# Attention plus linear attention on one core: loads in order of use, the last output projection accumulated early, a kept PSUM bank, VectorE steps kept back, and new step prices in the program's own scheduler

## The chip, the cores and the metric

The kernel runs on one core of one Trainium2 chip. The metric is device time in microseconds (us), the median of several executions. Faster or slower needs 2%. A core has five engines with separate instruction streams: TensorE (PE, matmuls into PSUM), VectorE (DVE), ScalarE (ACT), GpSimd (Pool) and SyncE (SP, which here issues loads and stores). The program divides PSUM into eight banks of 128 x 512 fp32.

## The reference, cut to what matters

```
def _A_ref(x, wqkv, wo):                      # softmax attention, 32 heads of 16
    qkv = (x @ wqkv) ...                      # x: 2048 x 512
    p = softmax(einsum("bhqd,bhkd->bhqk", q, k) * Dh**-0.5)
    o = einsum("bhqk,bhkd->bhqd", p, v)
    return o @ wo
def _B_ref(x, wqkv, wo):                      # linear attention with phi(t) = elu-like map
    kv = einsum("bhsd,bhse->bhde", phi(k), v); z = sum_s phi(k)
    return ((phi(q) @ kv) / (phi(q) @ z)) @ wo
g = sigmoid((x * gate_w).sum(-1, keepdims=True))
return g * a + (1 - g) * b
```

Softmax attention needs 32 x 2048 x 2048 exponentials. They come as 2048 tiles of 128 keys by 512 queries of one head.

## The kernel before

The program writes its own schedule. While it is being built, a small scheduler keeps a clock for each engine, prices each step, and appends instructions to the engines' streams in the order that its clocks suggest. Each stream keeps the order in which it was appended, and its steps wait for those of other engines by semaphores. So a wrong price does not slow an instruction down; it puts it at a place where something else has to wait for it.

There are 32 rounds (a quarter of the queries, four heads at a time). In a round, PE makes score tiles, ACT takes exponentials of three and two tiles in turn, and PE multiplies the results with V into one accumulating bank.

```
gsets = [(0, 1, 2), (3, 4)]                   # PSUM banks of ACT's tiles: three, then two
op(AC, lambda: nc.scalar.activation(PT[:, slot, 0:512 * n], ps[...], ACT.Exp, scale=SCALE), ...)
cur_units[0] = 64 * last[0] + 4 * last[1] + last[2] + 1    # progress: ACT's tiles only, 64 a round
```

VectorE takes some blocks of four tiles (one key block) off ACT. It evicts scores from banks 5 and 6 to integers, then computes the exponential by four chain steps on 128 x 2048 elements; PE multiplies three partial results with V:

```
op(DV, ... tensor_scalar(Lb[...], src, S1A, S1B, op0=ALU.mult, op1=ALU.add), cost=0.158 + 0.533 * n)   # n = 1 or 2 tiles
CH = [0.685, 0.685, 1.216, 0.685]             # the four chain steps (and, and, bf16 multiply, add)
def op(E, ...):                               # how VectorE is priced
    if E is DV:
        ev = E.add(fn, ..., cost=cost - 0.035, lag=0.035)
```

Everything else (projections for K, V, Q, the linear attention, the gate, the output projections) are tasks that use the same two banks 5 and 6 and start when the progress reaches their number `nb`. The gate ends in sixteen tiny copies, and an output projection is eight matmuls into one bank and an eviction:

```
for j in range(4):
    for a in range(4):
        op(DV, ... tensor_copy(gv[32*j:32*j+32, :, a], g0[32*a:32*a+32, :]), ..., cost=0.08)
def t_out(qc, q):                             # ops_: 4 products of part B, then 4 of part A
    for h in range(4):
        yield ("pe", rd, ..., 2)
        pe([mm(BK[b], ops_[k][0], ops_[k][1], start=(k == 0), stop=(k == 7)) for k in (2*h, 2*h+1)], ...)
    op(DV, ... tensor_copy(outt[:, sl, :], BK[b]), ..., cost=0.69)
add(("out", qc, q), t_out(qc, q), ..., max(17.2 + 3.0*qc + 3.0, 8*qc + 8.1) + 0.3*q if qc < 3 else 31.9, ...)
```

Where PE would stand idle by the scheduler's clock, it issues filler matmuls on a buffer of zeros (`sb_warm`), meant to keep PE's clock up.

The softmax here doesn't subtract the row's maximum and nothing guards it: scores larger than these inputs give would overflow.

## Time and profile before

| | before |
|---|---|
| median of three runs | 797.72 us (797.4 to 798.54) |
| span of the profiled run | 800.8 us |
| ACT busy | 764.0 us |
| first exponential starts | 17.75 us |
| last exponential ends | 788.7 us |

The following lines are of the page of the kernel before: span, busy time of each engine, the chain of waits by engine, and three groups of instructions (line, engine, operation, output <- inputs, count, then busy us and mean ns, then idle time just before them and what ended it). PEld are PE's weight loads; ACTq and SPq, here and below, are the loads and stores that ACT and SP issue.

```profile
span 800.8 us, 18062 instructions
...
PE 745.8 (93%) x7910; PEld 229.4 (29%) x7969; DVE 693.0 (87%) x979; ACT 764.0 (95%) x694; POOL 7.6 (1%) x35
...
ACT 84%; PE 8%; DVE 4%; issue 2%; DMA 1%; ACTq 0%; DVEq 0%
...
L840 ACT ACTIVATE sb_PT<-ps 128x1536 bf16<-128x1536 f32 (+1 forms) x659 | 757.0, 1413 | 14.7 <-PE ps L363 14.5
...
L1061 DVE TENSOR_SCALAR sb_Lb<-ps 128x512 uint16<-128x512 f32 (+1 forms) x282 | 256.4, 910 | 61.3 <-PE ps L363 57.6
...
L1088 DVE TENSOR_TENSOR sb_Xb<-sb_Xb,sb_Lb 128x2048 bf16<-128x2048 bf16 x100 | 121.6, 1216 | 0.0
```

ACT is busy from the first exponential to the last with few gaps, and the chain that ended last runs through it for 84% of the span. L840 are the exponentials (L363, in the lines below, is the helper that every matmul goes through); their idle time (14.5 us behind PE) contains the 6.3 us before the first. L1088 runs once in each of VectorE's blocks, so its count, 100, is the number of blocks. L1061 is the score eviction that opens them: VectorE stands 57.6 us waiting for PE there.

Three places outside the steady stream cost time. The first is the start (timeline: start, duration, engine, line, operation, count, and in brackets the idle time before it and its releaser):

```profile
1.81 7.00 ACTq L307 DMA_DIRECT2D sb_OT<-in_A_wqkv_dram  x2
...
12.26 3.57 PE L363 MATMUL ps<-sb_xT,sb_OT 128*128 128x512 bf16 x8 [6.03 <-DMA sb_OT<-in_A_wqkv_dram]
...
17.75 19.53 ACT L840 ACTIVATE sb_PT<-ps 128x1536 bf16<-128x1536 f32 x17 [6.29 <-PE ps L363]
```

The first K projection waits until 12.26 us for two small weight tiles (they borrow the space of `sb_OT`); issuing those two loads took ACT's queue 7.0 us. The second place is the tail, from the timeline of the end:

```profile
768.88 19.85 ACT L840 ACTIVATE sb_PT<-ps 128x1536 bf16<-128x1536 f32 x17
...
789.98 0.59 PE L363 MATMUL ps<-sb_phiK,sb_OT 128*128 128x512 bf16 x2
...
792.09 0.60 PE L363 MATMUL ps<-sb_phiK,sb_OT 128*128 128x512 bf16 x2 [1.52 <-DVE sb_OT L947]
...
797.91 0.69 DVE L647 CAST sb_wA<-ps 128x512 bf16<-128x512 f32 x1 [1.03 <-PE ps L363]
```

The last exponential ends at 788.7 us. Then VectorE normalizes (`sb_OT` is done at 792.0 us), and only after that PE runs most of the last four projections, with an eviction behind each. The third place is two groups of gaps in ACT's stream, here one of them in ACT's timeline:

```profile
50.62 1.02 ACT L840 ACTIVATE sb_PT<-ps 128x1024 bf16<-128x1024 f32 x1 [1.97 <-PE ps L363]
52.40 1.45 ACT L840 ACTIVATE sb_PT<-ps 128x1536 bf16<-128x1536 f32 x1 [0.76 <-PE ps L363]
```

### The profile page before, as it was taken

What the parts mean: (1) busy time and instruction counts of PE and PEld (TensorE: products, weight loads), DVE (VectorE), ACT (ScalarE), POOL (GpSimd) and SP (SyncE); (2) the same over time, 40 slices, a digit from 0 to 9 for tenths busy, and PEclk for the clock granted to TensorE, in tenths of its full rate; (3) what the DMA queues carried; (4) which work ended last, traced back from release to release, by engine and by line L of the source; (5) the groups of instructions that cost most, each with busy time, mean ns of one, the idle gap of its engine ahead of it and who ended that gap; (6) DMA issues with size and microseconds to landing.
All of it is one profiled execution on the core that took longest, in us unless ns stands there. A gap on an engine that the chain in (4) does not pass through costs nothing.

```text
span 800.8 us, 18062 instructions
## 1 busy us (share of the span) xinstructions
PE 745.8 (93%) x7910; PEld 229.4 (29%) x7969; DVE 693.0 (87%) x979; ACT 764.0 (95%) x694; POOL 7.6 (1%) x35
## 2 busy tenths in 40 slices
PE   6989999999999999999999999999999999999997
PEld 2422322222222222232222223222322332233222
DVE  3278899999999989998989999987889899799995
ACT  1989999999999999999999999998999999999993
POOL 3000000000000000000000000000000000000000
PEclk9999999999999999999999999997999999999999
DMA  9000000000000000102001000000001000100000
GB/s 231 20 1 8 2 7 2 8 2 8 1 4 6 2 7 2 35 2 56 5 1 61 2 8 12 17 29 7 13 17 30 11 14 16 34 8 14 16 1 27
DMA packets 30782, 14.93 MB, mean 19 GB/s; under 512 B 18544, under 2 KB 30704, under 8 KB 30704
## 3 DMA queue, kind: packets, MB, share of 16 engines
q1 hardware_dynamic: 26512, 11.95, 5.7%
q10 hardware_dynamic: 4192, 1.84, 1.1%
q8 instruction: 62, 1.02, 0.5%
q14 instruction: 16, 0.13, 0.0%
HBM read 6.55 MB, written 2.10 MB: 11 GB/s over the span
## 4 chain that ended last, share of the span: by engine, by line
ACT 84%; PE 8%; DVE 4%; issue 2%; DMA 1%; ACTq 0%; DVEq 0%
ACT sb_PT L840 82%; PE ps L363 8%; ACT sb_ebuf L529 2%; DVE sb_Lb L1061 1%; DMA sb_OT<-in_A_wqkv_dram 1%; DVE sb_gT L521 0%; DVE sb_Xb L1082 0%; DVE sb_Xb L1088 0%; DVE sb_U L928 0%; DVE sb_Eb L1085 0%; DVE sb_phiK L533 0%; DVE sb_Lb L1091 0%; ACTq L307 0%; DVE sb_rden L940 0%; DVE sb_OT L947 0%
## 5 line engine op out<-in xcount | busy, mean ns | idle before, releaser
L840 ACT ACTIVATE sb_PT<-ps 128x1536 bf16<-128x1536 f32 (+1 forms) x659 | 757.0, 1413 | 14.7 <-PE ps L363 14.5
L363 PE MATMUL ps<-sb_QP,sb_KT 32*128 32x512 bf16 x2048 | 307.3, 387 | 27.6 <-ACT sb_PT L840 17.2
L1061 DVE TENSOR_SCALAR sb_Lb<-ps 128x512 uint16<-128x512 f32 (+1 forms) x282 | 256.4, 910 | 61.3 <-PE ps L363 57.6
L363 PEld LDWEIGHTS ps<-sb_QP,sb_KT 32*128 32x128 bf16 x2048 | 76.7, 91 | 289.2 <-ACT sb_PT L840 225.0
L363 PE MATMUL ps<-sb_PT,sb_V 128*17 128x512 bf16 x1648 | 156.1, 387 | 1.4 <-ACT sb_PT L840 1.1
L363 PE MATMUL ps<-sb_warm 128*17 128x512 bf16 (+8 forms) x2190 | 154.4, 344 | 1.6 <-POOL sb_dummy L387 1.3
L1088 DVE TENSOR_TENSOR sb_Xb<-sb_Xb,sb_Lb 128x2048 bf16<-128x2048 bf16 x100 | 121.6, 1216 | 0.0
L1082 DVE TENSOR_SCALAR sb_Xb<-sb_Lb 128x2048 uint16<-128x2048 uint16 x100 | 68.7, 687 | 1.3
L1091 DVE TENSOR_SCALAR sb_Lb<-sb_Lb 128x2048 uint16<-128x2048 uint16 x100 | 68.5, 685 | 0.0
L1085 DVE TENSOR_SCALAR sb_Eb<-sb_Lb 128x2048 uint16<-128x2048 uint16 x100 | 68.3, 683 | 0.0
L363 PEld LDWEIGHTS ps<-sb_warm 128*17 128x17 bf16 (+1 forms) x2193 | 50.3, 90 | 58.0 <-issue 31.3
L363 PEld LDWEIGHTS ps<-sb_PT,sb_V 128*17 128x17 bf16 x1648 | 37.4, 87 | 97.7 <-issue 90.5
L363 PE MATMUL ps<-sb_Lb,sb_V 128*17 128x512 bf16 x400 | 39.2, 383 | 0.1
L363 PE MATMUL ps<-sb_Xb,sb_V 128*17 128x512 bf16 x400 | 39.0, 381 | 0.1
L363 PE MATMUL ps<-sb_Eb,sb_V 128*17 128x512 bf16 x400 | 39.0, 380 | 0.0
L363 PE MATMUL ps<-sb_xT,sb_wA 128*128 128x512 bf16 x89 | 26.8, 382 | 4.3 <-issue 1.9
L928 DVE STREAM_TRANSPOSE sb_U<-ps 128x512 f32<-128x512 f32 x32 | 22.7, 709 | 4.3 <-PE ps L363 4.1
L529 ACT ACTIVATE sb_ebuf<-ps 128x512 bf16<-128x512 f32 x32 | 25.3, 791 | 0.0
L363 PE MATMUL ps<-sb_wA,sb_xT 128*128 128x128 bf16 (+1 forms) x128 | 20.4, 285 | 2.7 <-DVE sb_Lb L1061 2.7
L453 DVE CAST sb_KT<-ps 128x512 bf16<-128x512 f32 x16 | 11.0, 686 | 9.8 <-PE ps L363 9.7
L363 PE MATMUL ps<-sb_phiK,sb_OT 128*128 128x512 bf16 x63 | 17.7, 382 | 1.7 <-DVE sb_OT L947 1.5
L363 PE MATMUL ps<-sb_wBx,sb_xT 128*128 128x512 bf16 x52 | 16.1, 382 | 2.2 <-issue 1.4
(79 smaller groups left out, 303.1 us busy)
## 6 DMA issues: line engine op xcount, KB each, us to landing
out_dram<-sb_wA SPq DMA_DIRECT2D x16, 128.0 KB, 1.7
sb_QP<-sb_QT SPq DMA_DIRECT2D x120, 16.0 KB, 1.8
sb_xnat<-in_A_x_dram ACTq DMA_DIRECT2D x2, 512.0 KB, 5.2
sb_wA<-in_A_wqkv_dram SPq DMA_DIRECT2D x2, 512.0 KB, 6.6
sb_wBx<-in_B_wqkv_dram SPq DMA_DIRECT2D x2, 512.0 KB, 5.9
sb_xnat<-in_A_x_dram SPq DMA_DIRECT2D x2, 512.0 KB, 3.9
sb_phiK<-sb_wA SPq DMA_TRANSPOSE x64, 2.2
sb_wA<-in_A_wqkv_dram ACTq DMA_DIRECT2D x1, 512.0 KB, 6.2
```

Source lines behind the costliest of these rows:

```text
L363: return lambda: nc.tensor.matmul(o, lhsT=l, rhs=r, start=start, stop=stop, skip_group_check=sg)
L453: op(DV, lambda: nc.vector.tensor_copy(KT[:, t8, 512 * t:512 * (t + 1)], BK[b]), reads=[r_bk[b]], writes=[r_KT[t8][t]], cost=0.69)
L529: op(AC, lambda: nc.scalar.activation(ebuf[:, s, :], BK[b], ACT.Exp), reads=[r_bk[b]], writes=[r_e[s]], cost=0.48)
L840: op(AC, lambda: nc.scalar.activation(PT[:, slot, 0:512 * n], ps[:, 512 * set_[0]:512 * (set_[0] + n)], ACT.Exp, scale=SCALE), reads=wr, w ...
L928: op(DV, lambda: nc.vector.transpose(U[:, par, :], acc), reads=[r_acc], writes=[r_U[par]], cost=0.71)
L1061: op(DV, lambda: nc.vector.tensor_scalar(Lb[:, sl, 512 * k:512 * (k + n)], src, S1A, S1B, op0=ALU.mult, op1=ALU.add), reads=[r_bk[b] for b ...
L1082: op(DV, lambda: nc.vector.tensor_scalar(X, L, 0x7F, 0x3F00, op0=ALU.bitwise_and, op1=ALU.bitwise_or), reads=[rl], writes=[rx], cost=CH[0])
L1085: ev = op(DV, lambda: nc.vector.tensor_scalar(E_, L, 0xFF80, None, op0=ALU.bitwise_and), reads=[rl], writes=[re_], cost=CH[1])
L1088: ev = op(DV, lambda: nc.vector.tensor_tensor(xb, xb, lb, ALU.mult), reads=[rx, rl], writes=[rx], cost=CH[2])
L1091: ev = op(DV, lambda: nc.vector.tensor_scalar(L, L, float(EXP_SH), None, op0=ALU.add), reads=[rl], writes=[rl], cost=CH[3])
```

## The change

Its intent is fivefold. (1) What the first exponential needs (a quarter of x, two 128-column weight tiles) is loaded first, each part under its own semaphore, and two memsets on VectorE are put off until after the first K and Q. (2) The last four output projections may accumulate all products but the last before the last normalization, and half of them are evicted by ACT. (3) When a task is due, VectorE's blocks leave one of the two banks free. (4) A chain step is kept back while VectorE's next score tile is in the making, so that it can fill the wait. (5) VectorE's steps get new prices: shorter pitch, with a delay between dependent steps. Due times of second-round work move as well, the gate among them (from progress 0.6 to 1.9), and the wait for the gate moves from the end of a round into the normalization. The diff, cut to its core:

```
-                ev = E.add(fn, _deps_for(E, reads, writes), cost=cost - 0.035, lag=0.035)
+                ev = E.add(fn, _deps_for(E, reads, writes), cost=max(cost - 0.084, 0.05), lag=min(0.084, cost - 0.05))
... (and 0.034 us between dependent steps of one engine)
-        for hh in range(2):
-            dma(xnat[:, 8 * hh:8 * hh + 8, :], ..., E=AC)             # two loads of 512 KB
-        dma(wA0[:, 0], ..., "w0", writes=[r_wA0], E=AC)
-        dma(wA0[:, 1], ..., "w0", writes=[r_wA0], E=AC)
+        load_xn(0, AC, 3.0)                                           # 256 KB
+        dma(wA0[:, 0], ..., "w0k", writes=[r_wA0[0]], E=AC, lat=4)
+        dma(wA0[:, 1], ..., "w0q", writes=[r_wA0[1]], E=AC, lat=4.5)
+        load_xT(0, 0, 3.6); load_xT(0, 1, 4.9) ...                    # the rest behind, on SP
-        op(DV, lambda: nc.vector.memset(QP[:], 0.0), ...)             # memsets at the start
-        op(DV, lambda: nc.vector.memset(V[:]...[:, :, Dh:Dh + 1], 1.0), ...)
...
             for h in range(4):
+                last = qc == NQC - 1 and h == 3
+                for kk in ([[6], [7]] if last else [[2 * h, 2 * h + 1]]):
+                    if kk == [7]:
+                        yield ("wait", ("pair", 8 * qc + 7))          # the last normalization
...
+            if qc == NQC - 1 and q % 2:
+                op(AC, lambda: nc.scalar.copy(outt[:, sl, :], BK[b]), ...)
...
+            if not held and pressed():                                # a due task waits for a bank
+                free = free[1:]
...
-            add(("V1", tb), t_v1(tb), 0.9 + 0.05 * (15 - tb), 0.45 + 0.06 * (15 - tb), pre=XT)
-        add(("gate",), t_gate(), 0.6, 0.5, pre=XT)
+            add(("V1", tb), t_v1(tb), V1D + 0.05 * (15 - tb), V1N + V1S * (15 - tb), pre=XT)   # .7, .3, .05
+        add(("gate",), t_gate(), GD, GN, pre=XT)                                            # 1.9, 1.5
...
         need(("Q", 0, 0))
+        op(DV, lambda: nc.vector.memset(QP[:, 1:3], 0.0), ...)
+        op(DV, lambda: nc.vector.memset(V[:]...[:, :, Dh:Dh + 1], 1.0), ...)
...
+            if apos[0] >= NR - 1 and dst["cur"] is None and progress() > TAILP:   # 31.5
+                maxhold[0] = 2
...
+                elif dst["cur"] is not None and lastd[0] and len(chainq) < 2:
+                    cands.append((max(now, DV.clock + CHG), 0.6, 0.0, chain_op, None))
```

## The prediction

> **What bounds the kernel.** ScalarE's exponentials: busy table, ACT 764 of 800.8 us; chain of waits, 82% the 659 exponentials. A three-plus-two pair of score tiles occupies ACT for 2.26 us (timeline, 770 to 782 us); a tile costs 0.459 us (757.0 us for 1648). VectorE computes the other 400 tiles, as 100 blocks of four. Time can come from four places: before the first exponential (17.75 us), after the last (788.7 to 800.8 us), ACT's gaps between (8.4 us), or more blocks on VectorE (each takes 4 x 0.459 = 1.84 us from ACT).
>
> **Start.** PE waits 6.0 us for two small weight tiles behind two 512 KB loads; issuing them blocks ACT's queue for 7.0 us, and K starts at 12.26 us. The change loads the first quarter of x and each weight under its own semaphore, the rest behind. It frees VectorE's masks from Pool's chain (4.6 us wait). I expect data at about 6 us, K and Q at half clock as now (0.43 us a matmul), the first exponential at about 11 us. The Trainium skill (DMA: Bandwidth & Descriptors, Issuing engines are not separate DMA queues) says SP's and ACT's loads interleave on the same 16 engines, so bytes ahead matter, not the issuer; this trace can't yet show it. Worth 6.5 us, all critical.
>
> **Tail.** Transpose and normalization (789.2 to 792.0 us) stay. Then come 16 output matmuls with four 0.69 us evictions until 798.6 us, and the last store. With seven of eight products accumulated ahead, four matmuls remain and two pairs of evictions, ACT beside DVE: worth 4.5 us.
>
> **Gaps.** ACT loses 4.2 us at 48 to 56 us and 3.9 us at 550 to 564 us. Both follow a hole in PE's work (2.7 us behind the gate's copies, 3.24 us on DVE; 1.4 us), and the granted clock then is 0.5. The Trainium skill (TensorE: Matmul & The Clock Gate, What's actually happening) puts such halving after an idle window of about 3.4 us; these holes are shorter, though work around them is thin. The kept bank and later gate should remove part; the gate's copies are still scheduled too cheap (0.08 against 0.2 us). I take 3 us.
>
> **VectorE's share.** DVE waits 57.6 us for PE before score evictions, some 50 us of it in the steady part. Holding chain steps back fills those waits. The scheduler's new pitch for DVE steps (0.60 and 1.13 us) equals the trace's; the old (0.65 and 1.18) was slow, so it should claim more. If 30 us of waits are filled, at 5.2 us of DVE a block plus 1.84 us of shortening, 30/7.0 = 4 more blocks: 8 us. Kept banks give some back as single evictions (0.69 us for one tile, 1.22 for two).
>
> **Sum.** 6.5 + 4.5 + 3 + 8 = 22 us: 775.7 us, range 766 to 787. Faster by over 2% (below 781.8 us): 0.74; same 0.25; slower 0.01.
>
> **What would show it.** First exponential at 10 to 12 us; last exponential to end 7.5 instead of 12.1 us; ACT gaps under 6 us; 103 to 105 blocks (count of the 128x2048 multiply), score evictions waiting 20 to 35 us for PE.
>
> **What would make it wrong.** Blocks not rising, claims being limited by banks or PE (93% busy); new half-clock stretches; the second round's V, K or Q late because their weights load last; first loads landing after 6 us.

## The result, and the profile after

The changed kernel took 792.27 us (median of four, 791.6 to 792.87), the kernel before in the same rounds 798.13 us (797.4 to 798.81). The ratio is 0.9927, with a 95% interval of 0.9909 to 0.9944: 0.7% faster, "same" by the 2% rule, and outside the predicted range. Here and below a ratio is fast runs alone, set against runs of the other kernel in the same rounds, so not quite the ratio of the medians quoted.

The same lines of the page after:

```profile
span 790.4 us, 17903 instructions
...
PE 743.7 (94%) x7815; PEld 227.3 (29%) x7877; DVE 701.7 (89%) x1009; ACT 760.6 (96%) x692; POOL 7.6 (1%) x35
...
ACT 73%; PE 16%; DVE 7%; issue 3%; DMA 1%; SPq 0%
...
L874 ACT ACTIVATE sb_PT<-ps 128x1536 bf16<-128x1536 f32 (+1 forms) x655 | 752.3, 1420 | 16.6 <-PE ps L364 16.0
...
L1115 DVE TENSOR_SCALAR sb_Lb<-ps 128x512 uint16<-128x512 f32 (+1 forms) x302 | 264.8, 878 | 47.8 <-PE ps L364 46.0
...
L1142 DVE TENSOR_TENSOR sb_Xb<-sb_Xb,sb_Lb 128x2048 bf16<-128x2048 bf16 x103 | 125.1, 1214 | 0.0
```

103 blocks instead of 100, and a shorter wait of the score evictions. But ACT's share of the chain fell from 84 to 73% and PE's rose from 8 to 16%: more of what ended last went through PE. The start, in the timeline after:

```profile
1.21 1.08 ACTq L308 DMA_DIRECT2D sb_OT<-in_A_wqkv_dram  x2
...
6.59 1.89 PE L364 MATMUL ps<-sb_xT,sb_OT 128*128 128x512 bf16 x8 [0.89 <-DMA sb_xT<-in_A_x_dram]
...
9.76 3.71 ACT L874 ACTIVATE sb_PT<-ps 128x1536 bf16<-128x1536 f32 x3 [5.94 <-PE ps L364]
...
12.70 0.48 DVE L1241 MEMSET sb_V<- 128x512 bf16 x1 [1.70 <-issue]
...
14.52 1.02 ACT L874 ACTIVATE sb_PT<-ps 128x1024 bf16<-128x1024 f32 x1 [1.05 <-PE ps L364]
```

The same two weight loads are issued in 1.08 us instead of 7.0, K's eight matmuls start at 6.59 us and take 1.89 us (12.26 and 3.57 us before), and the first exponential starts at 9.76 us. But after three exponentials ACT stands 1.05 us: VectorE's put-off memset of V's ones column ends only at 13.2 us, and the first V eviction and PE queue behind it. Gaps of ACT in the second round, in its timeline, and the same stretch by windows of 5 us (busy us and count of each engine, then the granted PE clock, 1.00 being full, then DMA share and GB/s):

```profile
94.10 2.36 ACT L874 ACTIVATE sb_PT<-ps 128x1536 bf16<-128x1536 f32 x2 [1.64 <-PE ps L364]
97.44 2.52 ACT L874 ACTIVATE sb_PT<-ps 128x1536 bf16<-128x1536 f32 x2 [0.97 <-PE ps L364]
101.51 2.53 ACT L874 ACTIVATE sb_PT<-ps 128x1536 bf16<-128x1536 f32 x2 [1.56 <-PE ps L364]
104.89 11.40 ACT L874 ACTIVATE sb_PT<-ps 128x1536 bf16<-128x1536 f32 x10 [0.85 <-PE ps L364]
```

```profile
90.00:95.00 5.00, 2.95 (x24) 0.73 (x24) 4.43 (x19) 3.37 (x4) 0.00 (x0) 0.92 0.00 0
95.00:100.00 5.00, 4.11 (x22) 0.76 (x21) 3.66 (x7) 3.94 (x4) 0.00 (x0) 0.50 0.00 0
100.00:105.00 5.00, 5.00 (x36) 0.97 (x36) 4.30 (x6) 2.59 (x3) 0.00 (x0) 0.55 0.01 3
```

That is the gate stall of the kernel before, at another place: a hole in PE's work first (2.95 us busy of 5), then ten microseconds at half clock in which PE is busy throughout or nearly so and ACT starves. Of ACT's 5.0 us, 1.64 stand directly behind the hole, the rest in the half-clock stretch. The tail, in the timeline after:

```profile
764.25 14.15 ACT L874 ACTIVATE sb_PT<-ps 128x1536 bf16<-128x1536 f32 x13 [0.63 <-PE ps L364]
...
779.87 0.81 PE L364 MATMUL ps<-sb_phiK,sb_OT 128*128 128x512 bf16 x3
...
781.98 0.39 PE L364 MATMUL ps<-sb_phiK,sb_OT 128*128 128x512 bf16 x1 [1.30 <-DVE sb_OT L983]
782.21 1.03 PE L364 MATMUL ps<-sb_phiK 128*128 128x512 bf16 x4
...
786.52 1.03 PE L364 MATMUL ps<-sb_phiK,sb_OT 128*128 128x512 bf16 x4
787.59 0.59 ACT L664 CAST sb_wA<-ps 128x512 bf16<-128x512 f32 x1 [2.87 <-PE ps L364]
```

Only the first of four projections was accumulated ahead. After the normalization PE still runs 25 matmuls, against 26 before. The last exponential ends at 778.4 us and the program at 790.4 us.

The span is summed up in the next table. "Before again" is a second profile of the kernel before, from the experiments; the first one was a slow execution (802.6 us, while the timed runs of those rounds took 797.4 to 798.8 us; over all rounds, 10 of the 26 timed runs took over 800 us). Gaps are ACT's idle stretches before exponentials after the first one, as its timeline lists them.

| us | first profile of before | before again | after | after minus before again |
|---|---|---|---|---|
| until the first exponential | 17.75 | 18.32 | 9.76 | -8.6 |
| exponentials, busy | 757.0 | 756.1 | 752.3 | -3.8 |
| ACT's gaps | 8.2 | 4.35 | 10.1 | +5.7 |
| last exponential to the end | 12.1 | 12.1 | 12.0 | -0.1 |
| the rest (other ACT work) | 5.7 | 5.8 | 6.3 | +0.4 |
| span | 800.8 | 796.7 | 790.4 | -6.3 |

So the start delivered more than expected, the extra blocks about half, the tail nothing, and the gaps took back two thirds of the start.

### The profile page after: what moved, and what is told of

The parts are those of the page before. It is cut to its first block, busy times and chain, and to the rows that moved or that the text cites. A ratio compares the mean times of both kernels' runs of the same rounds, so it can differ in the third digit from the quotient of the medians.

```text
span 790.4 us, 17903 instructions
## 1 busy us (share of the span) xinstructions
PE 743.7 (94%) x7815; PEld 227.3 (29%) x7877; DVE 701.7 (89%) x1009; ACT 760.6 (96%) x692; POOL 7.6 (1%) x35
## 4 chain that ended last, share of the span: by engine, by line
ACT 73%; PE 16%; DVE 7%; issue 3%; DMA 1%; SPq 0%
ACT sb_PT L874 71%; PE ps L364 16%; DVE sb_Lb L1115 2%; ACT sb_ebuf L542 2%; DVE sb_Xb L1142 1%; DVE sb_Xb L1136 1%; DMA sb_xT<-in_A_x_dram 1%; DVE sb_Eb L1139 0%; DVE sb_Lb L1145 0%; DVE sb_gT L534 0%; DVE sb_Tn L979 0%; DVE sb_OT L983 0%; DVE sb_U L964 0%; DVE sb_QP L482 0%; DVE sb_phiK L546 0%
## 5 line engine op out<-in xcount | busy, mean ns | idle before, releaser
L874 ACT ACTIVATE sb_PT<-ps 128x1536 bf16<-128x1536 f32 (+1 forms) x655 | 752.3, 1420 | 16.6 <-PE ps L364 16.0
L364 PE MATMUL ps<-sb_QP,sb_KT 32*128 32x512 bf16 x2048 | 312.1, 387 | 25.9 <-ACT sb_PT L874 13.3
L1115 DVE TENSOR_SCALAR sb_Lb<-ps 128x512 uint16<-128x512 f32 (+1 forms) x302 | 264.8, 878 | 47.8 <-PE ps L364 46.0
L364 PE MATMUL ps<-sb_warm 128*17 128x512 bf16 (+8 forms) x2074 | 147.0, 341 | 1.6 <-POOL sb_warm L402 1.3
L1142 DVE TENSOR_TENSOR sb_Xb<-sb_Xb,sb_Lb 128x2048 bf16<-128x2048 bf16 x103 | 125.1, 1214 | 0.0
L1136 DVE TENSOR_SCALAR sb_Xb<-sb_Lb 128x2048 uint16<-128x2048 uint16 x103 | 70.7, 686 | 1.4
L1139 DVE TENSOR_SCALAR sb_Eb<-sb_Lb 128x2048 uint16<-128x2048 uint16 x103 | 70.3, 683 | 0.0
L364 PEld LDWEIGHTS ps<-sb_warm 128*17 128x17 bf16 (+1 forms) x2077 | 48.2, 91 | 51.6 <-issue 27.0
L364 PE MATMUL ps<-sb_Eb,sb_V 128*17 128x512 bf16 x412 | 40.9, 388 | 0.2 <-DVE sb_Eb L1139 0.2
L364 PE MATMUL ps<-sb_xT,sb_wBx 128*128 128x512 bf16 x56 | 17.4, 383 | 1.5 <-issue 1.0
```

The source lines that it names most:

```text
L364: return lambda: nc.tensor.matmul(o, lhsT=l, rhs=r, start=start, stop=stop, skip_group_check=sg)
L1115: op(DV, lambda: nc.vector.tensor_scalar(Lb[:, sl, 512 * k:512 * (k + n)], src, S1A, S1B, op0=ALU.mult, op1=ALU.add), reads=[r_bk[b] for b ...
L1136: op(DV, lambda: nc.vector.tensor_scalar(X, L, 0x7F, 0x3F00, op0=ALU.bitwise_and, op1=ALU.bitwise_or), reads=[rl], writes=[rx], cost=CH[0])
L1139: ev = op(DV, lambda: nc.vector.tensor_scalar(E_, L, 0xFF80, None, op0=ALU.bitwise_and), reads=[rl], writes=[re_], cost=CH[1])
L1142: ev = op(DV, lambda: nc.vector.tensor_tensor(xb, xb, lb, ALU.mult), reads=[rx, rl], writes=[rx], cost=CH[2])
```

## The experiments

All runs gave correct results. Each is an edit of the changed kernel unless it says otherwise.

### A second profile of the kernel before

> The kernel before, unchanged, for a second profile. Theory: the profile I predicted from was itself about 4 us slower than the kernel's usual run (span 800.8 us where most runs last 797 to 799 us in all), and its half-clock stretch at 550 to 564 us, 3.9 us of ScalarE gaps, was an accident of that execution. Then this profile has a span near 796 us, the gap at 48 to 56 us again, and little or no gap near 550 us; gaps in all about 4.5 us. Rival: the stretch belongs to the schedule; then it is there again and the span is near 800 us.

Measured: 798.49 us, span 796.7 us. The gaps at 51 to 57 and 70 us are there again (4.35 us in all), and the one at 550 to 564 us is not. The two profiles are of one program, and both have the same hole in PE's work just before 550 us. Here are PE's line at its end and two windows, first of the first profile, then of the second.

```profile
549.66 1.02 PE L363 MATMUL ps<-sb_QP,sb_KT 32*128 32x512 bf16 x5 [1.38 <-ACT sb_PT L840]
...
550.00:555.00 5.00, 5.00 (x38) 0.90 (x33) 4.40 (x7) 4.52 (x5) 0.00 (x0) 0.50 0.02 3
555.00:560.00 5.00, 5.00 (x44) 1.10 (x40) 2.67 (x3) 3.15 (x3) 0.00 (x0) 0.50 0.00 0
```

```profile
550.21 0.61 PE L363 MATMUL ps<-sb_QP,sb_KT 32*128 32x512 bf16 x5 [1.37 <-ACT sb_PT L840]
...
550.00:555.00 5.00, 4.33 (x47) 1.23 (x47) 4.93 (x9) 5.00 (x6) 0.00 (x0) 1.00 0.02 5
555.00:560.00 5.00, 5.00 (x71) 2.01 (x68) 5.00 (x6) 5.00 (x6) 0.00 (x0) 1.00 0.00 0
```

The same 1.4 us hole was followed by half clock in one execution and by full clock in the other; ACT lost 3.9 us behind it in the first and nothing in the second. So here it is the halved clock, not the hole itself, that costs the time; what decides whether it comes is not shown. It follows also that my reading of 8.2 us of gaps before was too high by 3.9 us for an execution like the second one. Such a stretch is not rare, though: two of the profiles below have one like it, at 557 to 564 us (3.3 us of gaps) and at 566 to 576 us (4.0 us). Counted in windows of 1 us, half clock comes in these profiles in stretches of about 3.4 us or a multiple of that: 3.4 behind the gate's copies before, 10.2 behind them after, 13.7 here (ends cut off by the program's end, and one run at another clock, below, left out).

### The loads alone

Everything but the loads, the masks and the memsets undone: old prices, old due times, no kept bank, no held steps, old tail.

```
-                elif dst["cur"] is not None and lastd[0] and len(chainq) < 2:
+                elif False:
-            if not held and pressed():
+            if False:
... (old op() prices, old nb and due numbers, need(("gate",)) back in round_end, one matmul group a step and DVE evictions in t_out)
```

> The changed kernel with everything undone except the order of loads, the masks off Pool's chain, and the memsets put off: the scheduler's old costs and due times, no kept bank, no held chain steps, the old tail. Theory A (the start is worth its full 8 us wherever else nothing changes): first exponential at 9.8 us and a ratio to before of 0.990 to 0.992. Theory B (part of the early start is given back at once, because the memset of V's ones column now runs in front of the first V eviction and PE waits behind it): ScalarE gaps of 1 to 2 us between 13 and 16 us, and a ratio of 0.992 to 0.995. Blocks on VectorE 99 or 100 in either.

Measured: 823.3 us (820.62 to 825.8), ratio 1.0308 (1.0279 to 1.0337). The first exponential starts at 9.66 us, as expected, and the kernel is 25 us slower. Both theories missed. ACT's gaps are 31.5 us, nearly all in two stretches: 12.4 us between 46 and 94 us, where the gate's copies and then forced V and K projections hold PE up; and 17.6 us after 290 us, 9.4 of them behind this line, PE's wait for a reload of x that had not landed (then two of the windows behind it):

```profile
395.88 1.89 PE L365 MATMUL ps<-sb_phiK,sb_xnat 128*128 128x512 bf16 x4 [2.64 <-DMA sb_xnat<-in_A_x_dram]
...
395.00:400.00 5.00, 4.12 (x16) 0.90 (x17) 0.69 (x1) 1.08 (x2) 0.00 (x0) 0.50 0.43 105
400.00:405.00 5.00, 5.00 (x16) 0.63 (x12) 1.84 (x3) 3.23 (x3) 0.00 (x0) 0.50 0.00 0
```

The clock stays halved for 20 us there. Its mean over the whole run is 0.967, where the kernel before has 0.987 to 0.998 in most runs. Against the second profile of the kernel before, the span of 821.5 us is accounted for: 8.7 us less before the first exponential, 27.2 us more of gaps, and 6.3 us more of exponentials (762.4 us, with 99 blocks). An earlier start is not worth its 8 us by itself here: the whole order behind it shifts, and the shifts cost more than the start saves.

### The loads, with the due times and the kept bank given back

As the run before, with `V1D`, `K1D`, `GD` and their like, the moved wait for the gate, and `pressed()` of the changed kernel.

> The run with the loads alone, plus two parts of the change given back: the new due times of second-round work (V, K, Q, gate) and the kept bank; old prices, no held steps, old tail. The built program has 100 blocks. Theory (the loads alone lost 25 us because the earlier start brings the second round's forced work, then gate and V and K together, into one place; the new due times and the bank are what makes the early start pay): gaps fall from 31.5 us to 10 to 15 us, ratio 0.995 to 1.003. Rival (the loss came from elsewhere, such as the stall at 393 to 416 us behind a reload of x): gaps between 40 and 95 us stay near 13 us or those after 290 us stay near 14 us, and the ratio is above 1.015.

Measured: 799.3 us (794.24 to 802.79), ratio 0.9978 (0.993 to 1.0026). Gaps are 13.8 us, 0.8 us of them between 40 and 95 us and 3.3 us after 290 us. That is as the theory said: with the new due times and the bank, the early start stops losing. Which of the parts did it is not shown, since they came back together. It doesn't win anything yet: gaps and the lower clock still eat it up. The profile is of the slowest of the four runs, and its first exponential starts at 11.39 us instead of 9.66, because K's eight matmuls took 3.57 us in it.

### The last projections made eligible

```
-                add(("out", qc, q), ..., ... if qc < 3 else 31.9, ...
+                add(("out", qc, q), ..., ... if qc < 3 else 31.6 if q < 1 else 31.9, ...
+            if acc_round[0] >= NR:
+                for t in tasks:
+                    t.nb = -1
-                    if n >= 3:                          # in two places: candidates offered at once
+                    if n >= (3 if acc_round[0] < NR else 6):
```

> The changed kernel, with the last four output projections made eligible: one from progress 31.6, the others as soon as the last round's accumulation is emitted, instead of all at 31.9. Theory: the tail won nothing because progress counts ScalarE's tiles only and stops at 31.75 when VectorE has four blocks of the last round, so 31.9 is never reached and three of four projections stand behind the first one's last product in PE's order. Then the last exponential to the end falls from 12.0 us to 7.5 to 10 us and the ratio is 2 to 4 us (0.003 to 0.005) below the changed kernel's 0.9927. Rival: PE is the limit of the tail whatever the order (32 matmuls at 0.216 us are 6.9 us); then it falls by under 2 us.

Measured: 790.56 us (787.64 to 793.56), ratio 0.9896 (0.9857 to 0.9934). The last exponential to the end takes 9.46 us instead of 12.0. The end in the timeline:

```profile
783.34 1.46 PE L364 MATMUL ps<-sb_phiK,sb_OT 128*128 128x512 bf16 x6
784.62 0.59 ACT L664 CAST sb_wA<-ps 128x512 bf16<-128x512 f32 x1 [4.47 <-PE ps L364]
...
786.73 0.59 ACT L664 CAST sb_wA<-ps 128x512 bf16<-128x512 f32 x1 [1.53 <-DVE sb_wA L670]
```

Three of four projections are now accumulated ahead, and their closing products follow one another (the last three of the six matmuls of the first line). The cause of the missing gain in the changed kernel is thereby shown: progress counts ACT's tiles, 64 a round; with four blocks (16 tiles) of the last round on VectorE (the changed kernel's trace has 48 matmuls on ACT's tiles in that round) it ends at 31 + 48/64 = 31.75, and tasks that wait for 31.9 become eligible only when nothing else is left. By then the wait for the normalization stood in PE's stream in front of the other three. The gain is 2.5 us and not 4.5: PE has 32 matmuls to run at 0.216 us, of which 25 still run after the last exponential, without a pause from 780.96 us on, and 11 after the normalization. So PE itself limits part of the tail, as the rival said, though it expected under 2 us. The ratio alone would not show the gain, since the intervals overlap. The profiled run also lost 1.75 us at the start (first exponential at 11.51 us; K's matmuls took 3.57 us again), which hides most of the gain in its span of 789.6 us.

### The gate's copies at their measured price

```
-                       reads=[r_g0], writes=[r_gT], cost=0.08)
+                       reads=[r_g0], writes=[r_gT], cost=0.284)
```

> The changed kernel, with the gate's sixteen copies given a cost near the measured 0.2 us each in the scheduler (0.284 with its lag) instead of 0.08. Theory: the stall at 91 to 105 us comes from the scheduler placing PE work behind VectorE as if the copies took 0.8 us when they take 3.24 us, PE runs empty for 1.9 us, its clock is halved for some 10 us, and ScalarE loses 5.0 us. Then the gaps between 85 and 110 us fall from 5 us to under 2 us, and the ratio by 0.003 to 0.006. Rival: the hole has another cause (the copies occupy VectorE for 3.24 us whatever the plan); gaps stay at 4 to 5 us and the ratio within 0.002.

Measured: 788.22 us (785.54 to 789.33), ratio 0.9865 (0.984 to 0.9889), 0.006 under the changed kernel's. The copies in VectorE's timeline, and the windows:

```profile
89.66 3.24 DVE L534 COPY sb_gT<-sb_g 32x16 f32<-32x16 f32 x16
...
90.00:95.00 5.00, 4.38 (x32) 1.11 (x24) 4.43 (x20) 5.00 (x6) 0.00 (x0) 1.00 0.00 0
95.00:100.00 5.00, 4.64 (x40) 1.27 (x39) 3.86 (x7) 5.00 (x5) 0.00 (x0) 1.00 0.05 13
100.00:105.00 5.00, 5.00 (x45) 1.39 (x43) 5.00 (x8) 5.00 (x6) 0.00 (x0) 1.00 0.07 17
```

VectorE still spends the same 3.24 us on the copies, at nearly the same moment. But PE's stream now has other work there than work that needs VectorE, so PE's hole (1.89 us; now 0.53 at most), the halved clock and ACT's 5.0 us are gone. It was the price and not the occupation. The order of the rest changed too: 104 blocks, and a new gap of 2.65 us at 339 us. This profile is of the fastest of the four runs and has no half clock anywhere, where the changed kernel's has 20.5 us, so the gain is not the gate's stall alone.

### The same price in the kernel before

> The kernel before, with only the gate's sixteen copies priced near their measured 0.2 us each. If mispriced copies are the cause of the first stall of the kernel before too (4.2 us at 48 to 56 us, clock halved after it), that stall goes, and gaps fall from 4.35 us to under 2 us, ratio 0.994 to 0.997. Rival: the changed order makes stalls elsewhere of the same size or larger (every edit shifts the whole order): ratio within 0.003 of 1 or above, with gaps at another place.

Measured: 808.21 us (805.09 to 814.67), ratio 1.0081 (1.0048 to 1.0115): 0.8% slower, as the rival said. The profile is of the slowest run, 814.67 us. PE's longest pause behind the copies falls from 2.70 to 0.63 us, and ACT's gap of 1.97 us there goes. But the clock is halved all the same, for 6.8 us instead of 3.4:

```profile
50.00:55.00 5.00, 5.00 (x24) 0.95 (x25) 3.60 (x7) 3.68 (x4) 0.00 (x0) 0.56 0.00 0
```

So the gaps at 51 to 57 us fall only from 3.5 to 2.3 us, and new ones stand at 83 to 99, 121, 213 to 220 and 491 to 495 us, 17.6 us in all, with a stretch at 566 to 576 us among them. In both programs the right price takes away the hole behind the copies; only in one did the half clock go with it. The rest of the order happened to be good there, so the result of the experiment before can't be put down to the gate alone. A single right price doesn't make a good order.

### Old prices; no held steps; no kept bank

Three runs, each with one part of the change undone: the old lines of `op` and `add`; `elif False:` for the rule that holds steps; `if False:` for the kept bank.

> The changed kernel with the scheduler's old prices of VectorE steps (0.65 and 1.18 us pitch, no dependence between steps), all else kept. The built program has 99 blocks, so the 3 to 4 extra blocks come from the prices and not from holding chain steps. Theory (a block more is worth 1.84 us of ScalarE): exponentials' total longer by about 7 us than the changed kernel's, so a ratio near 1.000 to 1.003 if the gaps stay at 10 us. Rival (gaps move by more than the blocks are worth): the ratio lies outside that by more than 4 us, and the difference is in ScalarE's gaps and the half-clock time.

> The changed kernel without the rule that keeps chain steps back, all else kept. The built program has 102 blocks. Theory of my prediction (holding steps is what fills VectorE's waits): the wait of score evictions on PE rises from 46 us to 55 us or more, and the time by 4 us or more. Rival (the prices did most of it): the wait rises by under 5 us, one block less costs 1.8 us, ratio 0.993 to 0.998, unless the gaps move.

> The changed kernel without the kept bank, all else kept. The built program has 102 blocks. Theory: without the bank, due tasks (V, K, Q, phi) come late and PE stands behind them; gaps of ScalarE rise from 10 us to 15 us or more, half-clock time rises above 20 us, and the ratio is above 1.000. Rival: the kept bank costs VectorE single evictions and saves nothing; then the number of one-tile evictions falls from 192 towards 164 and the time falls.

| | ratio (95%) | blocks | eviction's wait | exponentials | gaps |
|---|---|---|---|---|---|
| changed kernel | 0.9927 (0.9909 to 0.9944) | 103 | 46.0 | 752.3 | 10.1 |
| old prices | 1.0052 (1.0009 to 1.0095) | 99 | 56.7 | 760.3 | 14.4 |
| no held steps | 0.9941 (0.989 to 0.9991) | 102 | 47.1 | 754.0 | 11.3 |
| no kept bank | 0.9976 (0.9932 to 1.0019) | 102 | 48.3 | 752.6 | 15.1 |

The medians of the three runs are 804.22, 795.07 and 798.41 us. These are the lines of the score evictions' wait, from the waits views of the run without held steps and of the one with old prices (us in total, times, longest); the changed kernel's 46.0 us stand in its page above:

```profile
DVE sb_Lb L1115 <- PE ps L364: 47.1, 78, 1.6
```

```profile
DVE sb_Lb L1116 <- PE ps L365: 56.7, 102, 3.7
```

The extra blocks come from the prices. With them undone there are four blocks fewer, exponentials take 8 us more, and the wait is back at 57 us. The ratio lies 0.002 above the theory's range, with 4.3 us more of gaps. Holding steps back changes the wait by 1.1 us and one block, and its ratio can't be told from the changed kernel's: the theory of my prediction missed, and the rival held. Without the kept bank the ratio is 0.005 higher, in gaps (15.1 against 10.1 us), though the intervals overlap; the expected "above 1.000" is not reached, and half-clock time is 17 us, not above 20 (the changed kernel has 20.5). The rival's fewer single evictions did come (180 against 192), without a gain.

### Three mends together

The tail's eligibility, the gate's price, and the two memsets back in VectorE's idle time before the first K:

```
+        op(DV, lambda: nc.vector.memset(V[:]...[:, :, Dh:Dh + 1], 1.0), ..., cost=2.2)     # before ACT's first table load
+        op(DV, lambda: nc.vector.memset(QP[:, 1:3], 0.0), ..., cost=0.9)
-        (the same two after need(("Q", 0, 0)))
```

> The changed kernel with three mends together: the last projections made eligible (2.5 us by its own run), the gate's copies at their measured cost (4.9 us), and the two put-off memsets moved back into VectorE's idle time before the first K (2.2 to 5.4 us). Theory: the last takes away the 1.05 and 0.41 us gaps near 15 us, and the three add up: 2.5 + 4.9 + 1.4 = 8.8 us under the changed kernel, a ratio of about 0.982 and a median near 783.5 us. Rival: each edit shifts the whole schedule, so they do not add: 0.984 to 0.990.

Measured: 781.56 us (780.94 to 782.14), ratio 0.9767 (0.9725 to 0.9809; "unclear" by the 2% rule), the kernel before at 799.59 us in these rounds. The memset now runs early, and ACT goes on from its first exponential without the two gaps near 15 us:

```profile
3.87 0.48 DVE L428 MEMSET sb_V<- 128x512 bf16 x1 [1.69 <-issue]
...
9.82 13.66 ACT L876 ACTIVATE sb_PT<-ps 128x1536 bf16<-128x1536 f32 x12 [5.99 <-PE ps L364]
```

Gaps are 3.45 us in all, the clock is 1.000 in the profiled run, there are 104 blocks, and the eviction's wait is 34.1 us. The three ratios added would have given 0.982; the sum is better by 0.005, in medians by 2 us. No run was made to test that surplus, but the profiles place most of it. Against the profile with the gate's price alone (783.7 us of span, no half clock) the three mends save 2.8 us of tail and 1.45 us of gaps, near the 2.5 and 1.4 expected. That profile was of the fastest run; the other three, from which the sum was mostly reckoned, took 2.2 to 3.8 us longer at a mean clock of 0.993 to 0.996.

### A rule for the remaining gap, and the copies on Pool

In the three mends' profile, 2.65 us of the gaps stand at 337 us. PE runs fourteen projection matmuls there while weighted sums wait and all ten buffers of probabilities are full. The rule puts weighted sums first in that state; the second run also moves the gate's copies to Pool.

```
+            stuck = ca is not None and ca[0] >= INF
-    key=lambda c: (..., c[1] if c[1] <= 0.7 else 1 if pmode[c[1]] == mode[0] else 2, c[1])
+    key=lambda c: (..., c[1] if c[1] <= 0.7 else 0.8 if stuck and c[1] in (2, 3) else 1 if ... else 2, c[1])
```

> The three mends, plus a rule for the 2.65 us gap at 337 us: there PE runs fourteen projection matmuls in a row (3.2 us) while sixteen weighted-sum matmuls wait, because with all ten probability buffers full the scheduler sees no exponential to protect; now weighted sums go first in that state. The built program has 103 blocks (104 without the rule). Theory: the gap goes (2.65 us), one block less costs 1.8 us, net 0 to 2 us faster than the three mends: ratio 0.974 to 0.977. Rival: the shifted order brings a new stall: above 0.980.

> As the run before, with the gate's sixteen copies on Pool, which is idle, instead of VectorE at their measured cost. Theory: VectorE gains 3.2 us, about half a block, so at most 1 us faster; it also tells whether it was the price or the occupation of VectorE that mattered, since both give no stall. Rival: the copies on Pool come later than the plan says or slow VectorE's own reads; then a stall near 90 us returns. Ratio 0.972 to 0.978 by the theory.

Measured: 779.64 us (778.53 to 788.59), ratio 0.9762 (0.9705 to 0.9819), and 783.2 us (783.04 to 783.41), ratio 0.9782 (0.9762 to 0.9802); both are "unclear" by the 2% rule. The gap at 337 us is gone in both; neither can be told from the three mends. The first one's profile fell in its slowest run, which had a clock of 0.85 until about 440 us and 0.95 afterwards almost everywhere; its gaps are not compared. The ratio includes this run; the other three were at 0.998 to 1.000 and 778.5 to 779.7 us. The second one shows no stall near 90 us beyond 0.4 us, so copies off VectorE serve as well as copies rightly priced; but it has a new half-clock stretch at 750 us with 3.2 us of gaps, more than the 2.65 us that the rule took away.

## Why the prediction was wrong, point by point

The prediction said 775.7 us (766 to 787) and "faster by over 2%"; the kernel took 792.27 us.

- **What bounds the kernel: right.** Every difference in the table of spans is found at ACT: before its first exponential, in its count of tiles, in its gaps, or after its last.
- **The start ("Worth 6.5 us, all critical"): the size was low and "all critical" was wrong.** It was 8.6 us. The term that I mis-sized is "K and Q at half clock as now (0.43 us a matmul)": PE now waits 0.89 us for data before K instead of 6.03, and K's matmuls took 0.24 us each, which is 1.7 us of the difference. That does not always happen: in 2 of the 11 profiles with the new loads they took 0.45 us, and the first exponential came at 11.4 and 11.5 us. (In the first profile of the kernel before the clock is recorded as 1.00 at that place and only the matmuls' pace is half; in the second, half clock is recorded from 7 to 18 us.) No run tells whether the bytes ahead or the issuing engine made the loads late. Of the 8.6 us, 1.5 us were lost at once behind the put-off memset (the three mends got them back). And alone the new start loses 3%, since the order behind it shifts.
- **The tail ("with seven of eight products accumulated ahead, four matmuls remain"): this step failed.** I took the intent for the effect. 25 matmuls remained, because three of four projections were not eligible in time. (The "16 output matmuls" from which I started were a miscount as well: the trace of the kernel before has 26.) I had the numbers to see it: the threshold 31.9 was in the code, and so was a progress that doesn't count VectorE's tiles. Made eligible, the tail gives 2.5 us.
- **Gaps ("I take 3 us"): this step failed, with the wrong sign.** They grew by 5.7 us. I had even written that the gate's copies stayed underpriced, and still credited a gain for moving them: moved from progress 0.6 to 1.9, they made the same stall, 5.0 us instead of 3.5. And 3.9 us of the gaps that I counted on came and went from one execution to the next.
- **VectorE's share ("Holding chain steps back fills those waits", 30 us of them, 4 blocks, 8 us): mis-sized, and put down to the wrong part.** 8.5 us of waits were filled (54.5 to 46.0), 3 blocks were won, and the exponentials took 3.8 us less. The prices brought the blocks; holding steps brought at most one.
- **The sum.** I added four terms as if they were independent. Measured, in the same order: -8.6 - 0.1 + 5.7 - 3.8 = -6.8 us, with +0.4 of other work -6.3 us of span.
- Of what I listed as making it wrong, "new half-clock stretches" came true: 20.5 us of half clock in four stretches. Late V, K or Q of the second round did not show in the changed kernel; it did where the due times were old.

What stays open: why an edit of one price moves the gaps by -5 us in one kernel and +13 us in another, and why this change's order had the stalls at 428 to 453 us and 764 us. I can name the holes (0.96, 1.12 and 0.62 us) and the 3.4 us of halved clock behind each, not predict them.

## What to carry to other kernels

When a program orders its own instructions by a cost model, a step that is priced wrong by a factor costs more than its own time: the engine that waits in order runs empty, and if that is PE, its clock can halve: in these profiles for 3.4 to 20.5 us behind holes of 0.6 to 2.7 us, though not behind every one. So look in the trace for holes in PE's work behind which the granted clock falls, find the step that made each, and put its measured duration into the model, but measure each such mend on the chip, since the same one-line price made one kernel 0.6% faster and another 0.8% slower. And check that a threshold which is to trigger an optimization is reached at all: count the instructions behind it in the trace.

## What the Trainium skill lacked or had wrong

- TensorE: Matmul & The Clock Gate, What's actually happening, puts the halved clock after at least one idle window of about 3.4 us, and "Why this matters for your kernels" advises against idle gaps over about 3 us. Here half clock followed holes of 1.38, 1.89 and 2.64 us in thin work, and lasted 13.7, 10.2 and 20.5 us; it also came where no pause was longer than 0.63 us (6.8 us of it), and after a hole of 1.37 us in the program that had the 1.38 it did not. The page's own section on a second failure mode tells of short idles doing this, but gives no length. For a kernel with a full ScalarE the cost of those three was 3.9, 5.0 and 9.4 us.
- On the same page, What's actually happening has two clock states, and Seeing it yourself a third, 13/16, once three cores of a die run dense matmuls. One execution of a one-core kernel ran at a recorded 0.85, later 0.95, nearly throughout (788.6 us against 779.3 for the mean of its three other runs). What else the chip did then is not known.
- DMA: Bandwidth & Descriptors, Issuing engines are not separate DMA queues, says that the sequencer's time to initiate a DMA is usually small relative to the DMA itself. It held after the change (1.08 us for two loads); before it, the same two loads behind two of 512 KB kept ACT's queue for 7.0 us. The section doesn't say what can hold up issuing; that it was the loads in flight is likely, but no run tested it.
- No page that I read tells of this: the strided memset of V's ones column has a record of 0.48 us, but 1.68 to 1.70 us of VectorE's time in front of it have no releaser, wherever it stands in the program (before, after, three mends), so that it ends about 2.2 us after the step before it (11.0 to 13.2 us after). That the memset itself takes this time is likely, but not shown.
